# Linear attention and a gated FFN on one core: the next pair's k tiles join the projection burst, PSUM banks in shared pairs, and all transposes at the visit's end

## The chip, the cores and the metric

The kernel runs on one core of one Trainium2 chip. The metric is device time in microseconds for one execution, and the figure shown is the median of three. TensorE, VectorE, ScalarE, GpSimd and SyncE (which issues the DMAs here) each work through a list of instructions in order and wait for each other by semaphores. The profile calls them PE, DVE, ACT, POOL and SP; PEld is TensorE's weight load.

## What is computed

```python
def phi(x):
    proj = np.einsum('bhsd,df->bhsf', x, w_phi)
    proj = proj - np.max(np.abs(proj), axis=-1, keepdims=True)
    return np.concatenate([np.exp(proj), np.exp(-proj)], axis=-1)
q_p, k_p = (phi(q), phi(k))
kv = np.einsum('bhsf,bhsd->bhfd', k_p, v)
z = np.sum(k_p, axis=2)
num = np.einsum('bhsf,bhfd->bhsd', q_p, kv)
den = np.einsum('bhsf,bhf->bhs', q_p, z)[..., None] + 1e-06
attn = num / den                       # 8 batches, 8 heads, 576 tokens, 64 wide
...
h = x @ w_in                           # x: 4608 x 512, w_in: 512 x 2048
g = np.maximum(h, 0.0) + alpha * np.minimum(h, 0.0)
out = g @ w_out                        # 2048 x 512
```

There are 128 features, 256 with both signs. Everything is float32. The FFN's weights are float64, stored as pairs of words that the kernel decodes itself.

## The kernel before

**Pairs and visits.** Two heads of a batch form a pair, so there are 32 pairs. The work of a pair is cut into some 25 units (a projection, an exponential, a DMA), and a table, `places(i)`, gives each unit a number. Pair i's number plus i is the unit's place; all units of all pairs, of the FFN and of the weight decoding are sorted by place and issued in that order, which then stands on TensorE, SyncE, VectorE and ScalarE. GpSimd's order is free. The stretch between place i and i + 1 is called visit i here. The table's numbers are no times: what is fixed is the order alone.

**What TensorE does in a visit.** Of pair i: the projection of five tiles of tokens with q in them, for two heads (`project(1)`; the first of the five holds the last 64 rows of k and of q). Of pair i - 1: k_z (the sum z, by a product with ones), k_acc (kv, k features against v), the transposes of kv (`kv_turn`) and of the projected q (`q_turn`, three groups). Of pair i - 2: d (the denominator) and n (the numerator). Of pair i + 1: the projection of four k tiles (`project(0)`), behind n. From visit 9 on gemm steps of the FFN stand in between, each three matmuls (high by high, low by high, high by low, on tiles split into a rounded high part and a rest: L503 to L505 up, L509 to L511 down), and the four groups of transposes stand among those steps.

**The other engines.** VectorE takes the maximum of each projected tile over its features and subtracts it (L311, L312); this frees the PSUM bank. The part that is projected first (`pl`, two tiles 128 wide) is done ahead of the 1024-wide rest (`pj`). ScalarE takes exponentials (k: L320 and L325, q: L402 and L404), copies kv (ks), the turned kv (sf), d and n (s) out of PSUM, and does the activation of the FFN (r and g from h) and the rounding to a high part (gh); VectorE joins r and g (L240) and forms the low part (gl). VectorE inverts d; the reciprocals go to DRAM (`rec_out`), come back spread over partitions (`spread`), GpSimd multiplies (`finish`), and the result goes to x_d, from which the FFN fetches xr.

**The weights.** In the early visits one or two blocks of a weight are decoded per visit: fetched by SyncE (raww), scaled on ScalarE (L173), split on VectorE (L181 to L184), added on GpSimd, rounded and stored. `WA` holds the places of the two blocks within a visit.

**PSUM.** Eight banks while attention runs: `psf` two (h and o of the FFN; in the early visits, where there is no FFN, half of the turned q, and the k projection of pairs 0 and 1), `ps_pj` one tile of two banks (every other projection), `ps_kv` one (kv and z), `ps_m` three single banks, taken in turn by the two small projections, d, the two halves of n, the turned kv and turned q. A tile is given the next bank of its pool and waits until the bank's former tile has been read.

**After attention** a second pass over the tokens does the FFN's other 11 blocks of 128 features.

Of the kernel before, what the change touches and what calls it, by code (L numbers as in the profile page):

```python
# [36 lines left out]
W_BUFS = 2  # L37
RW_BUFS = 4
WN = 256
WA = (0.0040, 0.50)  # L40
W2A = 12.5
W2D = 0.70
G2_BUFS = 3
# [65 lines left out]
def fused_kernel(ctx: ExitStack, tc: tile.TileContext, kq, v, w_phi, w_in, w_out, alpha, out):  # L109
    nc = tc.nc  # L110
    act, dve, pool, pe = nc.scalar, nc.vector, nc.gpsimd, nc.tensor
# [94 lines left out]
    def decode_store(ff, z, o, n):  # L206
# [6 lines left out]
        scale=decode_scale,  # L213
# [50 lines left out]
    ones = cat.tile([P, 32], F32, name="ones")  # L264
    pool.memset(ones, 1.0)
    k4buf = []
    for n in range(2):
        k4 = cat.tile([P, 2, 2, FD], F32, name=f"k4_{n}")
# [3 lines left out]
    def attention_units(i):  # L272
        b, hp = divmod(i, NP)
        c = {}
# [9 lines left out]

        def project(ch):
            t = c["t", ch] = wk.tile([P, 2, 4 + ch, FD], F32, tag=f"t{ch}", name=f"t{i}_{ch}", bufs=1 + ch)
            dst, out, js = {}, [], [0, 1, 2, 3]
            if ch:
                js = [4] + js
                for h in range(2):  # L290
                    p1 = ps_m.tile([P, 1, 1, FD], F32, tag="m", name=f"pl{i}_{h}")
                    dst[h, 4] = p1[:, 0, 0]
                    out.append((slice(h, h + 1), slice(4, 5), p1))
            if ch == 0 and i < 2:
                for h in range(2):
                    p1 = psf.tile([P, 1, 4, FD], F32, tag="f", name=f"pj{i}_{ch}_{h}")
                    dst.update({(h, j): p1[:, 0, j] for j in range(4)})
                    out.append((slice(h, h + 1), slice(0, 4), p1))
            else:
                p2 = ps_pj.tile([P, 2, 4, FD], F32, tag="pj", name=f"pj{i}_{ch}")  # L300
                dst.update({(h, j): p2[:, h, j] for h in range(2) for j in range(4)})
                out.append((slice(0, 2), slice(0, 4), p2))
            for j in js:
                for h in range(2):
                    hs = slice(h * D, (h + 1) * D)
                    ts = slice((4 * ch + j) * P, (4 * ch + j + 1) * P)
                    pe.matmul(dst[h, j], lhsT=c["raw"][hs, ts], rhs=w_sb[hs], start=True, stop=True)  # L307
            for n, (hs, js, src) in enumerate(out):
                nh, nj = hs.stop - hs.start, js.stop - js.start
                m = wk.tile([P, nh, nj], F32, tag="m", name=f"m{i}_{ch}_{n}", bufs=4)  # L310
                dve.tensor_reduce(m, src, axis=AX.X, op=ALU.max, apply_absolute_value=True)  # L311
                dve.tensor_tensor(  # L312
                    t[:, hs, js], src, m.unsqueeze(3).broadcast_to([P, nh, nj, FD]), op=ALU.subtract
                )
# [39 lines left out]
                    )  # L354

        def k_z():
            c["kv"] = ps_kv.tile([P, 3, FD], F32, tag="kv", name=f"kv{i}")
            if i < ZP:
                zs = [c["x", 0][:, :, :, j, :] for j in range(4)] + [c["x", 1][:, :, :, 0, :]]
            else:  # L360
                zs = [c["z"]]
            for j, z in enumerate(zs):
                for g in range(4):
                    h, a = divmod(g, 2)
                    pe.matmul(  # L365
                        c["kv"][32 * g : 32 * g + 32, 2],
                        lhsT=ones,
                        rhs=z[:, a, h, :],
                        start=j == 0,
                        stop=j == len(zs) - 1,  # L370
                    )

        def kv_out():
            c["ks"] = st.tile([P, 3, FD], F32, tag="ks", name=f"ks{i}", bufs=1)
            act.copy(c["ks"], c["kv"])

        def kv_turn():
            ps = c["kt"] = ps_m.tile([P, 3, P], F32, tag="m", name=f"kt{i}")
            for j in range(3):
                pe.transpose(ps[:, j, :], c["ks"][:, j, :], ident)  # L380
# [5 lines left out]
        def q_turn(h):  # L386
            pp, tag = (psf, "f") if i < ZP - 1 and h < 2 else (ps_m, "m")
            ps = c["qt", h] = pp.tile([P, 2 if h == 2 else 4, P], F32, tag=tag, name=f"qt{i}_{h}")
            if h == 2:
                for g in range(2):  # L390
                    pe.transpose(ps[:, g, :], c["t", 1][:, g, 0, :], ident)
            else:
                for j in range(4):
                    pe.transpose(ps[:, j, :], c["t", 1][:, h, 1 + j, :], ident)  # L394

        def q_exp(h):
            ps = c["qt", h]
            if h == 2:
                c["qf"] = qp.tile([P, 2, 2, S], F32, tag="qf", name=f"qf{i}", bufs=QH_BUFS)
            for a, sg in enumerate((1.0, -1.0)):  # L400
                if h == 2:
                    act.activation(c["qf"][:, :, a, 4 * P :], ps[:, :, 64:], AF.Exp, scale=sg)  # L402
                else:
                    act.activation(  # L404
                        c["qf"][:, h, a, : 4 * P], ps.rearrange("p j f -> p (j f)"), AF.Exp, scale=sg
                    )

        def num():
            for u in range(2):
                ps = c["n", u] = ps_m.tile([P, HS], F32, tag="m", name=f"n{i}_{u}")  # L410
                for a in range(2):
                    for h in range(2):
                        pe.matmul(  # L413
                            ps[h * D : (h + 1) * D, :],
                            lhsT=c["st"][:, a, h * D : (h + 1) * D],
                            rhs=c["qf"][:, h, a, u * HS : (u + 1) * HS],
                            start=a == 0,
                            stop=a == 1,
                        )
# [49 lines left out]
        us = [  # L469
            (at["ld"], load),  # L470
            (at["lv"], load_v),
            (at["ka"], k_acc),
            (at["kz"], k_z),
            (at["ko"], kv_out),
            (at["kr"], kv_turn),
            (at["kc"], kv_copy),
            (at["n"], num),
            (at["d"], den),
# [9 lines left out]
        for n in range(2):  # L488
            us.append((at["p"][n], lambda n=n: project(n)))
        for n in range(3):  # L490
            us.append((at["ks"][n], lambda n=n: k_sum(n)))
            us.append((at["q"][n], lambda n=n: q_turn(n)))
# [231 lines left out]
    for ff in range(NB):  # L724
        t = T2 + ff * U2
# [75 lines left out]
```

## Time and profile before

| | us |
|---|---|
| median of three runs | 1140.24 |
| lowest, highest | 1139.62, 1142.58 |
| the profiled execution, its time | 1140.04 |
| its span | 1138.2 |
| TensorE busy | 1114.4 |
| VectorE busy | 634.0 |
| ScalarE busy | 561.1 |
| GpSimd busy | 213.9 |

The span is the time from the first to the last recorded instruction. An instruction's row gives its start, its duration, engine, line and operation, the tile written and those read, and how many like it were run together; in brackets stands the idle time before it and what ended that. TensorE's matmuls overlap, so the step from one start to the next is what one costs there. Early visits last about 10.6 us, late ones 16.5 us, of which the gemm steps are the larger half.

### The profile page before, as it was taken

To read this page: it belongs to the slowest core of one execution; us is meant where nothing else is said; L and a number is where in the kernel's file an instruction comes from. 1 tells how busy PE (TensorE), PEld (TensorE's weight loads), DVE (VectorE), ACT (ScalarE), POOL (GpSimd) and SP (SyncE) were. 2 spreads that over 40 slices of the span, in tenths; PEclk is the share of its full clock that TensorE was granted. 3 is DMA by queue.
4 is the path that set the end of the run, shared out by engine and by line. 5 is a ranking of instruction groups with operands and counts; after the bars stand their busy time and mean duration, and the time that the engine had idled before them with its cause. 6 is when DMAs were issued, how large, how long until landed. Compare 5 with 4: busy or idle time off the path is not lost.

```text
span 1138.2 us, 18351 instructions
## 1 busy us (share of the span) xinstructions
PE 1114.4 (98%) x7232; PEld 865.2 (76%) x7232; DVE 634.0 (56%) x978; ACT 561.1 (49%) x1149; POOL 213.9 (19%) x219
## 2 busy tenths in 40 slices
PE   6999999999999999999999999999999999999998
PEld 5766767777777777677778788888888888888886
DVE  7888957798687777836861342424242333333322
ACT  4777656666666765664543333333333333433332
POOL 1345332322424142243542000000000000000000
PEclk9999999999999999999999999999999999999999
DMA  5467264555556365466627030303030302112021
GB/s 190 147 186 219 68 194 143 172 164 183 162 167 195 99 211 167 146 202 219 227 65 246 32 111 1 111 1 111 1 111 1 111 1 75 37 33 79 1 74 37
DMA packets 74101, 133.68 MB, mean 117 GB/s; under 512 B 14624, under 2 KB 24480, under 8 KB 73376
## 3 DMA queue, kind: packets, MB, share of 16 engines
q1 hardware_dynamic: 71712, 122.48, 33.7%
q0 software_dynamic: 2016, 9.96, 2.5%
q8 instruction: 57, 0.93, 0.3%
q14 instruction: 28, 0.23, 0.1%
q10 hardware_dynamic: 288, 0.07, 0.0%
HBM read 93.92 MB, written 38.42 MB: 116 GB/s over the span
## 4 chain that ended last, share of the span: by engine, by line
PE 88%; DVE 6%; DMA 4%; ACT 2%; issue 1%; SPq 0%; DVEq 0%; ACTq 0%
PE h L503 11%; PE h L505 11%; PE h L504 11%; PE po L511 8%; PE po L509 8%; PE po L510 8%; PE kv L348 6%; PE n L413 5%; PE pj L307 5%; PE o L511 3%; PE o L509 3%; PE o L510 3%; PE d L431 2%; PE qt L394 2%; DMA xr<-x_d 2%; PE kv L365 1%
## 5 line engine op out<-in xcount | busy, mean ns | idle before, releaser
L240 DVE SCALAR_TENSOR_TENSOR g<-r,aln,g 128x512 f32<-128x512 f32 x144 | 111.7, 775 | 307.1 <-ACT g L236 306.9
L235 ACT ACTIVATE r<-h 128x512 f32<-128x512 f32 x144 | 86.5, 601 | 293.3 <-PE h L505 293.2
L127 DVE TENSOR_TENSOR gl<-g,gh 128x512 fp32r<-128x512 f32 x144 | 104.7, 727 | 67.6 <-ACT gh L123 67.1
L123 ACT CAST gh<-g 128x512 fp32r<-128x512 f32 x144 | 90.0, 625 | 85.6 <-DVE g L240 85.6
L236 ACT ACTIVATE g<-h 128x512 f32<-128x512 f32 x144 | 86.0, 598 | 1.0 <-DMA part_d<-os 1.0
L509 PE MATMUL po<-gh,wd 128*128 128x512 f32 x216 | 84.6, 392 | 0.7 <-ACT gh L123 0.7
L510 PE MATMUL po<-gh,wd 128*128 128x512 f32 x216 | 84.7, 392 | 0.0
L511 PE MATMUL po<-gl,wd 128*128 128x512 f32 x216 | 84.5, 391 | 0.0
L311 DVE TENSOR_REDUCE m<-pj 128x8 f32<-128x1024 f32 (+1 forms) x66 | 78.2, 1185 | 10.4 <-PE pj L307 10.3
L307 PE MATMUL pj<-w_sb,raw 64*128 64x128 f32 x1024 | 73.2, 283 | 9.8 <-DMA w_sb<-w_phi_dram 4.6
L307 PEld LDWEIGHTS pj<-w_sb,raw 64*128 64x128 f32 x1024 | 64.1, 192 | 23.3 <-issue 15.6
L189 POOL TENSOR_TENSOR aw<-ew,aw 128x256 f32<-128x256 f32 x64 | 56.6, 885 | 128.6 <-DVE ew L184 128.6
L312 DVE TENSOR_TENSOR t<-pj,m 128x1024 f32<-128x1024 f32 (+1 forms) x66 | 78.7, 1192 | 2.3
L509 PE MATMUL o<-gh,w 128*128 128x512 f32 x180 | 76.0, 422 | 2.6 <-ACT os L554 2.4
L463 POOL TENSOR_TENSOR s<-s,rr 128x576 f32<-128x576 f32 x32 | 48.5, 1517 | 145.3 <-DMA rr<-rec_d 127.7
L503 PE MATMUL h<-xh,w 128*128 128x512 f32 x180 | 75.8, 421 | 0.0
L511 PE MATMUL o<-gl,w 128*128 128x512 f32 x180 | 71.7, 399 | 3.6 <-DVE gl L127 3.4
L404 ACT ACTIVATE qf<-qt 128x512 f32<-128x512 f32 x128 | 68.4, 615 | 6.3 <-PE qt L394 6.3
L511 PE MATMUL po<-gl,w 128*128 128x512 f32 x180 | 69.7, 390 | 1.4 <-DVE gl L127 1.4
L505 PE MATMUL h<-xl,w 128*128 128x512 f32 x180 | 70.7, 393 | 0.0
L510 PE MATMUL o<-gh,w 128*128 128x512 f32 x180 | 70.6, 392 | 0.0
L504 PE MATMUL h<-xh,w 128*128 128x512 f32 x180 | 70.5, 392 | 0.0
(105 smaller groups left out, 2402.6 us busy)
## 6 DMA issues: line engine op xcount, KB each, us to landing
xr<-x_d SPq DMA_DIRECT2D x18, 1024.0 KB
raw<-kq_dram SPq DMA_DIRECT2D x31, 576.0 KB
v<-v_dram SPq DMA_DIRECT2D x32, 320.0 KB
w_d<-raww SPq DMA_DIRECT2D x38, 256.0 KB
rr<-rec_d SPq DMA_DIRECT2D x64, 144.0 KB
x_d<-s SPq DMA_DIRECT2D x32, 288.0 KB
part_d<-os SPq DMA_DIRECT2D x36, 256.0 KB
pt<-part_d SPq DMA_DIRECT2D x9, 1024.0 KB
```

What stands on the lines that cost most here:

```text
L123: return act.copy(dst, src)
L127: return eng.tensor_tensor(dst, src, f(hi), op=ALU.subtract)
L235: act.activation(st["r"], ps, AF.Relu, scale=-1.0)
L236: act.activation(st["g"], ps, AF.Relu)
L240: dve.scalar_tensor_tensor(g, st["r"], aln[:, ff : ff + 1], g, op0=ALU.mult, op1=ALU.add)
L307: pe.matmul(dst[h, j], lhsT=c["raw"][hs, ts], rhs=w_sb[hs], start=True, stop=True)
L503: pe.matmul(ps, lhsT=wt[0][:, ws], rhs=xh, start=n == 0, stop=False)
L504: pe.matmul(ps, lhsT=wt[1][:, ws], rhs=xh, start=False, stop=False)
L505: pe.matmul(ps, lhsT=wt[0][:, ws], rhs=xl, start=False, stop=n == NK - 1)
L509: pe.matmul(ps, lhsT=wt[2][:, ws], rhs=gh, start=first, stop=False)
L510: pe.matmul(ps, lhsT=wt[3][:, ws], rhs=gh, start=False, stop=False)
L511: pe.matmul(ps, lhsT=wt[2][:, ws], rhs=gl, start=False, stop=last)
```

## The change

Five things are changed; what is computed stays.

- `p`: the k projection of the next pair moves from behind n to right behind the q projection of this pair.
- PSUM: `ps_pj` gets two tiles of two banks, `ps_m` keeps one bank. The two tiles are taken in turn by the q projection, the next pair's k projection, n (both halves in one tile, so that one copy takes it out) and the turned q (or, in the early visits, the turned kv). Of the two small projections one goes to a fourth column of the kv bank, one to the bank of `ps_m`, which then also holds d and, in the late visits, the turned kv with the small part of the turned q (`kq`). The turned z goes to the fourth column of the kv bank.
- The transposes of kv and q (13) stand together behind n, in front of the visit's gemm steps.
- The q exponentials go by sign rather than by head, and earlier in the visit; VectorE's three sums of k features (`ks`) come behind both projections.
- `WA`: the second decode block of a visit moves from 0.50 to 0.0046, beside the first.

```diff
-WA = (0.0040, 0.50)
+WA = (0.0040, 0.0046)
...
-        p=(-0.9955 if early else -0.993, 0.0),
-        ke=(-0.26, 0.0011),
-        ks=(0.0015, 0.0022, 0.0026),
-        kz=1.0002,
-        ka=1.0012,
-        ko=1.0025,
-        kr=1.10,
-        kc=1.16,
-        q=(1.34, 1.50, 1.20),
-        qe=(1.46, 1.62, 1.28),
-        d=2.0004,
-        ds=2.0008,
-        n=2.005,
-        s=2.0055,
+        p=(-0.9998, 0.0),
+        kz=1.0004,
+        d=2.0006,
+        ka=1.0010,
+        n=2.0020,
+        kr=1.0030,
+        q=1.0034,
+        ds=2.0012,
+        ke=(-0.26, 0.0014),
+        ko=1.0022,
+        s=2.0028,
+        kc=1.0036,
+        qe=(1.0040, 1.0044, 1.0048) if early else (1.04, 1.30, 1.42),
+        ks=(0.02, 0.05, 0.08),
...
-    ps_m = ps_m_.enter_context(tc.tile_pool(name="ps_m", bufs=3, space=PSUM))
+    ps_m = ps_m_.enter_context(tc.tile_pool(name="ps_m", bufs=1, space=PSUM))
...
-    ps_pj = att.enter_context(tc.tile_pool(name="ps_pj", bufs=1, space=PSUM))
+    ps_pj = att.enter_context(tc.tile_pool(name="ps_pj", bufs=2, space=PSUM))
...
-                js = [4] + js
-                for h in range(2):
-                    p1 = ps_m.tile([P, 1, 1, FD], F32, tag="m", name=f"pl{i}_{h}")
...
+                kvb[i] = ps_kv.tile([P, 4, FD], F32, tag="kv", name=f"kv{i}")
+                p1 = ps_m.tile([P, 4, FD], F32, tag="m", name=f"pl{i}")
+                for h, t1 in enumerate((kvb[i][:, 3:4], p1[:, 0:1])):
+                    dst[h, 0] = t1[:, 0]
+                    out.append((slice(h, h + 1), slice(0, 1), t1.unsqueeze(1)))
+            p2 = ps_pj.tile([P, 2, 4, FD], F32, tag="pj", name=f"pj{i}_{ch}")
...
+            if i < ZP - 1:
+                c["kq"] = ps_pj.tile([P, 2, 4, FD], F32, tag="pj", name=f"kq{i}")[:, 0]
+            else:
+                c["kq"] = ps_m.tile([P, 4, FD], F32, tag="m", name=f"kq{i}")
             for j in range(3):
-                pe.transpose(ps[:, j, :], c["ks"][:, j, :], ident)
+                pe.transpose(c["kq"][:, j] if j < 2 else c["kv"][:, 3], c["ks"][:, j, :], ident)
...
-            act.copy(c["st"], c["kt"])
+            act.copy(c["st"][:, 0:2], c["kq"][:, 0:2])
+            act.copy(c["st"][:, 2], c["kv"][:, 3])
...
+            c["n"] = ps_pj.tile([P, 2, 512], F32, tag="pj", name=f"n{i}")
...
-            for u in range(2):
-                act.copy(c["s"][:, u * HS : (u + 1) * HS], c["n", u])
+            act.copy(c["s"].rearrange("p (u n) -> p u n", u=2), c["n"][:, :, :HS])
```

What the table of numbers makes of the order shows in two places. The first is TensorE at the start of visit 14; the number in a name is the pair, and h1_1_4 is a tile of the FFN. Before:

```order
L505 MATMUL h1_1_4_2486<-xl1_1_2050,w4_94 128x512
L307 MATMUL pl14_0_2492<-w_sb_73,raw14_2186 128x128
L307 MATMUL pl14_1_2493<-w_sb_73,raw14_2186 128x128
L307 MATMUL pj14_1_2494<-w_sb_73,raw14_2186 128x128 x8
L365 MATMUL kv13_2514<-z13_2338,ones_119 32x128 x4
L431 MATMUL d12_2519<-qf12_2409,sf12_2388 32x288 x8
L348 MATMUL kv13_2514<-xk13_2258,v13_2199 64x256 x8
L348 MATMUL kv13_2514<-k4_1_123,v13_2199 64x256 x2
L413 MATMUL n12_0_2552<-qf12_2409,sf12_2388 64x288 x4
L413 MATMUL n12_1_2557<-qf12_2409,sf12_2388 64x288 x4
L307 MATMUL pj15_0_2566<-w_sb_73,raw15_2377 128x128 x8
L503 MATMUL h1_1_4_2486<-xh1_1_2049,w4_94 128x512
```

And now:

```order
L302 MATMUL kv14_2432<-w_sb_73,raw14_2152 128x128
L302 MATMUL pl14_2433<-w_sb_73,raw14_2152 128x128
L302 MATMUL pj14_1_2434<-w_sb_73,raw14_2152 128x128 x8
L302 MATMUL pj15_0_2455<-w_sb_73,raw15_2337 128x128 x8
L362 MATMUL kv14_2432<-z13_2330,ones_119 32x128 x4
L436 MATMUL d12_2471<-qf12_2327,sf12_2322 32x288 x8
L343 MATMUL kv14_2432<-xk13_2204,v13_2160 64x256 x8
L343 MATMUL kv14_2432<-k4_1_123,v13_2160 64x256 x2
L419 MATMUL n12_2497<-qf12_2327,sf12_2322 64x288 x8
L380 MATMUL kq13_2510<-ident_67,ks13_2506 128x128 x2
L380 MATMUL kv14_2432<-ident_67,ks13_2506 128x128
L389 MATMUL kq13_2510<-ident_67,t13_1_2228 128x128 x2
```

The projection of pair 15's k tiles went from behind n to behind pair 14's projection, the transposes of pair 13 follow n at once, and pl14 and d12 are now tiles of one bank, as kv14 holds a small projection and then z13.

The second place is VectorE in visit 5, an early one: m is a maximum, t the subtracted projection, r9 the reciprocal of d, aw a weight block being split. Before:

```order
L311 TENSOR_REDUCE m5_1_1_831<-pl5_1_816 128x1
L312 TENSOR_TENSOR t5_1_814<-pl5_1_816,m5_1_1_831 128x128
L311 TENSOR_REDUCE m5_1_2_834<-pj5_1_817 128x8
L312 TENSOR_TENSOR t5_1_814<-pj5_1_817,m5_1_2_834 128x2x512
L450 RECIPROCAL r9_2_881<-d9_2_773 128x9
L181 TENSOR_SCALAR aw4_0_0_808<-aw4_0_0_808 128x256
```

And now:

```order
L307 TENSOR_TENSOR t5_1_799<-pl5_801,m5_1_1_816 128x128
L306 TENSOR_REDUCE m5_1_2_819<-pj5_1_802 128x8
L307 TENSOR_TENSOR t5_1_799<-pj5_1_802,m5_1_2_819 128x2x512
L306 TENSOR_REDUCE m6_0_0_832<-pj6_0_823 128x8
L307 TENSOR_TENSOR t6_0_822<-pj6_0_823,m6_0_0_832 128x1024
L455 RECIPROCAL r9_2_878<-d9_2_780 128x9
L181 TENSOR_SCALAR aw4_0_0_794<-aw4_0_0_794 128x256
```

The next pair's maximum and subtraction (m6_0, t6_0) now stand ahead of the reciprocal r9_2; before they stood behind it and behind the split of the weight block.

More of the change, by code (lines that the diff above doesn't have):

```diff
@@ L265, in fused_kernel @@
     pool.memset(ones, 1.0)
+    kvb = {}
     k4buf = []
@@ L286, in project @@
             t = c["t", ch] = wk.tile([P, 2, 4 + ch, FD], F32, tag=f"t{ch}", name=f"t{i}_{ch}", bufs=1 + ch)
-            dst, out, js = {}, [], [0, 1, 2, 3]
+            dst, out = {}, []
             if ch:
-                js = [4] + js
-                for h in range(2):
-                    p1 = ps_m.tile([P, 1, 1, FD], F32, tag="m", name=f"pl{i}_{h}")
[L292 to L303, printed above, removed]
+                kvb[i] = ps_kv.tile([P, 4, FD], F32, tag="kv", name=f"kv{i}")
[4 more added lines that the diff above has]
+            p2 = ps_pj.tile([P, 2, 4, FD], F32, tag="pj", name=f"pj{i}_{ch}")
+            dst.update({(h, ch + j): p2[:, h, j] for h in range(2) for j in range(4)})
+            out.append((slice(0, 2), slice(ch, ch + 4), p2))
+            for j in range(4 + ch):
                 for h in range(2):
@@ L356, in k_z @@
         def k_z():
-            c["kv"] = ps_kv.tile([P, 3, FD], F32, tag="kv", name=f"kv{i}")
+            if i + 1 not in kvb:
+                kvb[i + 1] = ps_kv.tile([P, 4, FD], F32, tag="kv", name=f"kv{i + 1}")
+            c["kv"] = kvb[i + 1]
             if i < ZP:
@@ L374, in kv_out @@
             c["ks"] = st.tile([P, 3, FD], F32, tag="ks", name=f"ks{i}", bufs=1)
-            act.copy(c["ks"], c["kv"])
+            act.copy(c["ks"], c["kv"][:, 0:3])
         def kv_turn():
-            ps = c["kt"] = ps_m.tile([P, 3, P], F32, tag="m", name=f"kt{i}")
+            if i < ZP - 1:
+                c["kq"] = ps_pj.tile([P, 2, 4, FD], F32, tag="pj", name=f"kq{i}")[:, 0]
+            else:
+                c["kq"] = ps_m.tile([P, 4, FD], F32, tag="m", name=f"kq{i}")
             for j in range(3):
-                pe.transpose(ps[:, j, :], c["ks"][:, j, :], ident)
+                pe.transpose(c["kq"][:, j] if j < 2 else c["kv"][:, 3], c["ks"][:, j, :], ident)
@@ L382, in kv_copy @@
         def kv_copy():
             c["st"] = st.tile([P, 3, P], F32, tag="sf", name=f"sf{i}")
-            act.copy(c["st"], c["kt"])
[L386 to L391, printed above, removed]
-            else:
+            act.copy(c["st"][:, 0:2], c["kq"][:, 0:2])
@@ new lines, in kv_copy, with q_turn @@
+            act.copy(c["st"][:, 2], c["kv"][:, 3])
+        def q_turn():
+            for g in range(2):
+                pe.transpose(c["kq"][:, 2 + g], c["t", 1][:, g, 0, :], ident)
+            if i < ZP - 1:
+                ps = [psf.tile([P, 1, 4, P], F32, tag="f", name=f"qt{i}_{h}") for h in range(2)]
+                c["qt"] = [(slice(h, h + 1), ps[h]) for h in range(2)]
+                qt = [p1[:, 0] for p1 in ps]
+            else:
+                p2 = ps_pj.tile([P, 2, 4, P], F32, tag="pj", name=f"qt{i}")
+                c["qt"] = [(slice(0, 2), p2)]
+                qt = [p2[:, h] for h in range(2)]
+            for h in range(2):
@@ L393, in q_turn, with q_exp @@
                 for j in range(4):
[L394 to L398, printed above, removed]
+                    pe.transpose(qt[h][:, j], c["t", 1][:, h, 1 + j, :], ident)
+        def q_exp(n):
+            if n == 0:
                 c["qf"] = qp.tile([P, 2, 2, S], F32, tag="qf", name=f"qf{i}", bufs=QH_BUFS)
[L400 to L406, printed above, removed]
+                for a, sg in enumerate((1.0, -1.0)):
+                    act.activation(c["qf"][:, :, a, 4 * P :], c["kq"][:, 2:4, 64:], AF.Exp, scale=sg)
+                return
+            a, sg = ((0, 1.0), (1, -1.0))[n - 1]
+            for hs, ps in c["qt"]:
+                act.activation(
+                    c["qf"][:, hs, a, : 4 * P], ps.rearrange("p h j f -> p h (j f)"), AF.Exp, scale=sg
+                )
@@ L408, in num @@
         def num():
+            c["n"] = ps_pj.tile([P, 2, 512], F32, tag="pj", name=f"n{i}")
             for u in range(2):
-                ps = c["n", u] = ps_m.tile([P, HS], F32, tag="m", name=f"n{i}_{u}")
                 for a in range(2):
```

4 lines of the change are left out of this document (2 added, 2 removed).

## The prediction

> **What bounds the kernel now.** I read the page first, then TensorE's own list of waits, then one late visit instruction by instruction.
>
> ```profile
> span 1138.2 us, 18351 instructions
> PE 1114.4 (98%) x7232; PEld 865.2 (76%) x7232; DVE 634.0 (56%) x978; ACT 561.1 (49%) x1149; POOL 213.9 (19%) x219
> L311 DVE TENSOR_REDUCE m<-pj 128x8 f32<-128x1024 f32 (+1 forms) x66 | 78.2, 1185 | 10.4 <-PE pj L307 10.3
> L312 DVE TENSOR_TENSOR t<-pj,m 128x1024 f32<-128x1024 f32 (+1 forms) x66 | 78.7, 1192 | 2.3
> ...
> PE o L511 <- DVE gl L127: 3.4, 5, 1.6
> PE d L431 <- ACT qf L404: 1.0, 2, 0.7
> ```
>
> TensorE is busy for 98% of the span, and its waits (total, times, longest) are small: 3.4 us on low halves, 1.0 us on d. VectorE's maximum and subtraction of a 1024-wide projection cost 1.2 us each, which is used below. Since TensorE sets the time, any new wait of it is paid in full, and only what shortens its own list of work is a gain. Here is visit 19 on TensorE:
>
> ```profile
> 276.27 0.49 PE L307 MATMUL pl<-w_sb,raw 64*128 64x128 f32 x4
> 276.59 1.06 PE L307 MATMUL pj<-w_sb,raw 64*128 64x128 f32 x16
> 277.58 0.43 PE L365 MATMUL kv<-z,ones 128*32 128x128 f32 x8
> 277.82 1.15 PE L431 MATMUL d<-qf,sf 128*32 128x288 f32 x16
> 278.91 1.95 PE L348 MATMUL kv<-xk,v 128*64 128x256 f32 x16
> ...
> 281.12 2.11 PE L413 MATMUL n<-qf,sf 128*64 128x288 f32 x16
> 283.16 1.16 PE L307 MATMUL pj<-w_sb,raw 64*128 64x128 f32 x16
> 284.25 0.50 PE L509 MATMUL o<-gh,w 128*128 128x512 f32 x1
> 284.58 0.39 PE L510 MATMUL o<-gh,w 128*128 128x512 f32 x1
> 284.81 0.39 PE L511 MATMUL o<-gl,w 128*128 128x512 f32 x1
> 285.05 0.49 PE L380 MATMUL kt<-ident,ks 128*128 128x128 f32 x3
> 285.29 0.48 PE L509 MATMUL o<-gh,w 128*128 128x512 f32 x1
> ...
> 287.68 0.60 PE L394 MATMUL qt<-ident,t 128*128 128x128 f32 x4
> 288.04 0.48 PE L509 MATMUL o<-gh,w 128*128 128x512 f32 x1
> ```
>
> The step from one start to the next is the price of a row, since the matmuls overlap.
>
> **The late visits' packing (visits 10 to 30, 21 of them).** By these starts the first projection burst costs 0.32 + 0.99 = 1.31 us, z 0.24, d 1.09, k_acc 2.21 (278.91 to 281.12), n 2.04, the next pair's projection 1.09. Put behind the first burst, the second projection costs 0.99 as its equal there does, 0.10 less than alone; n then goes straight into the transposes. The four groups of transposes are one of three (0.24, 285.05 to 285.29), two of four (0.36 each, 287.68 to 288.04) and one of two, which at the same 0.08 apiece makes 0.16: 1.12 us. Each also makes the next L509 step longer: after other work it is 0.33 (284.25 to 284.58), where a gemm step among its like takes 0.23 (284.58 to 284.81). Four such restarts are 0.40, 1.52 together. In the early visits, where 13 already stand in a row, they take 1.57 us (52.85 to 54.42, below), no less than the 1.52 here. What is saved is the 0.10 at the second projection and the restart of 0.10 behind it (284.25 to 284.58): before 1.09 + 0.10 + 1.52 = 2.71, after 0.99 + 1.57 + 0 to 0.10 for the one restart, 2.56 to 2.66. Were a transpose 0.09 in the row, as in the group of four, it would be 2.26. I take a saving near the first, 0.13 a visit: 21 x 0.13 = **-2.8 us** (ends 0.06 and 0.21 a visit, -1.3 and -4.4). The low-half waits of 3.4 us come about when a short run of gemm steps stands between transposes; longer runs give VectorE more time in some of them: **-1.0** (0 to -2).
>
> **The new wait.** The trace of before has no such wait. The pool of single banks ps_m goes from three banks to one. Before, a visit's two small projections (pl) and d took three banks, and the first to need an old one was n, 3.3 us later (277.82 to 281.12). Now pl and d lie in the same bank, and the other small tile lies in the kv bank, whose z columns TensorE writes next. So d cannot start until VectorE has taken the maximum of the second small tile and subtracted it. TensorE reaches z at burst start + 1.31 + 0.99 = 2.30 and d at 2.30 + 0.24 = 2.54. VectorE's end in before, with the burst's start on TensorE in the row ahead:
>
> ```profile
> 117.03 0.49 PE L307 MATMUL pl<-w_sb,raw 64*128 64x128 f32 x4
> 120.24 0.29 DVE L312 TENSOR_TENSOR t<-pl,m 128x128 f32<-128x128 f32 x1
> 134.93 0.49 PE L307 MATMUL pl<-w_sb,raw 64*128 64x128 f32 x4
> 138.51 0.29 DVE L312 TENSOR_TENSOR t<-pl,m 128x128 f32<-128x128 f32 x1
> 190.67 0.49 PE L307 MATMUL pl<-w_sb,raw 64*128 64x128 f32 x4
> 194.61 0.29 DVE L312 TENSOR_TENSOR t<-pl,m 128x128 f32<-128x128 f32 x1
> 309.31 0.49 PE L307 MATMUL pl<-w_sb,raw 64*128 64x128 f32 x4
> 312.62 0.29 DVE L312 TENSOR_TENSOR t<-pl,m 128x128 f32<-128x128 f32 x1
> 425.56 0.49 PE L307 MATMUL pl<-w_sb,raw 64*128 64x128 f32 x4
> 428.55 0.29 DVE L312 TENSOR_TENSOR t<-pl,m 128x128 f32<-128x128 f32 x1
> 442.08 0.49 PE L307 MATMUL pl<-w_sb,raw 64*128 64x128 f32 x4
> 446.45 0.29 DVE L312 TENSOR_TENSOR t<-pl,m 128x128 f32<-128x128 f32 x1
> ```
>
> End minus burst start: 3.50, 3.87, 4.23, 3.60, 3.28 and 4.66 us in visits 10, 11, 14, 21, 28 and 29. Less 2.54 these are waits of 0.96, 1.33, 1.69, 1.06, 0.74 and 2.12, together 7.9; with 0.05 each for the signal **+8.2 us**. The other visits end early enough or miss by 0.3 at most. Queued behind d on TensorE stand k_acc, n, the transposes and all gemm steps of the visit, so nothing fills the gap. What makes VectorE late is seen in visit 14:
>
> ```profile
> 189.53 2.04 ACT L325 ACTIVATE xk<-t 128x1024 f32<-128x1024 f32 x2
> 192.42 0.64 ACT L236 ACTIVATE g<-h 128x512 f32<-128x512 f32 x1
> 193.10 0.75 DVE L240 SCALAR_TENSOR_TENSOR g<-r,aln,g 128x512 f32<-128x512 f32 x1 [1.49 <-ACT g L236]
> ```
>
> VectorE stands 1.49 us for ScalarE's g, which is queued behind the k exponentials of 2.04 us; the small maxima stand behind that g in VectorE's order. After the change the same g stands ahead of the same small maxima, and the k exponentials at the same place ahead of it. The q exponentials move up, but their transposes now stand in front of all gemm steps, so the h tile that ScalarE works on comes up to 1.4 us later: the two cancel, and I keep the lateness. Ends: +4 (half of it goes) and +14 (0.3 more in each of the 21 visits).
>
> The Trainium skill ("Perfetto Trace Analysis", section Optimizing Tensor Performance, Matmuls) asks that independent matmul groups rotate through different PSUM banks, so that the evacuation of one overlaps the matmuls of the next. It speaks against going from three banks to one; read strictly it would charge every visit. By the rows only the late ones pay.
>
> **The early visits (0 to 8) and the start.** No gemm covers anything there, so the order on the other queues matters too.
>
> ```profile
> 43.84 0.49 PE L307 MATMUL pl<-w_sb,raw 64*128 64x128 f32 x4
> 48.98 0.32 SPq L453 DMA_DIRECT2D rec_d<-r  x1
> 52.85 0.55 PE L380 MATMUL kt<-ident,ks 128*128 128x128 f32 x3
> 54.42 0.49 PE L307 MATMUL pl<-w_sb,raw 64*128 64x128 f32 x4
> 58.95 0.44 ACT L173 ACTIVATE aw<-raww 128x256 f32<-128x256 f32 x1 [0.23 <-DMA raww<-w_in_dram]
> ```
>
> A visit takes 10.58 us (43.84 to 54.42). TensorE's part shrinks by 0.10 at the merged burst and 0.10 where k_acc runs into n: 6 x 0.2 = -1.2 for visits 3 to 8, and at the start, where the first pairs' banks are shared otherwise, about -0.4. Against it: the k projection's maximum and subtraction move ahead of the reciprocal on VectorE, so rec_d, issued at visit start + 5.14 (48.98), goes out after the small tiles (1.7 us) and twice 2.4 us (the two page rows), with the reciprocal at about + 6.75, 1.6 us later. SP's queue is in order: the fetch of raw behind rec_d, the spread and the weight fetch all shift by as much. The first weight tile lands 9.97 after rec_d (48.98 to 58.95), now at the next visit's start + 6.1 to 6.3 (6.75 + 9.97 less 10.4 to 10.6). ScalarE's scaling of both weight tiles (0.44 for the first) stands ahead of the d copy, the k exponentials and the kv copy, on which the transposes wait; these start at + 9.0 before (43.84 to 52.85) and at about + 8.8 now. That the two decode blocks of a visit now follow each other takes ScalarE and VectorE work out of the visit's middle and costs TensorE nothing while the first arrives in time. The sum of gain and delay could be -2.5 (the gain and half as much again) or +5 (0.8 in each of six visits); I take **0**, since the some 2.6 us left to ScalarE there are about what its pieces need (two scalings 0.4 each, an exponential pair and two copies).
>
> The second pass (after 35.4 on the table) has the same order on each engine and costs nothing new. The one n copy in place of two, and two copies of the turned kv in place of one, are off TensorE's path: they need to end before the q burst of the next visit, and until then TensorE has the gemm steps (284.25 onward) to do.
>
> **Sum:** -2.8 - 1.0 + 8.2 + 0 = +4.4 us on the profiled 1140.04. That execution is 0.2 under the median of the runs, 1140.24, so the forecast is **1144.6 us**.
>
> **The rivals.**
> A, the forecast: d waits for VectorE in the late visits. 1144.6, with 1142 to 1150 as its own range. Chance 0.45.
> B, VectorE is on time: the q exponentials, earlier by up to 0.2 of a visit, empty ScalarE's queue ahead of the k exponentials, and the small maxima start within 1.26 us of the burst (2.54 less the 1.13 that four pieces of 0.28 to 0.29 take, and 0.15 for the signals). For it: in visits not listed they do that already. Against it: in visit 14 ScalarE's queue is full from the h tiles, which come later now. Then -2.8 - 1.0 and the early -1.6: 1140.2 - 5.4 = 1134.8. It decides from half of the listed visits being on time onward. Chance 0.18; faster.
> C, half of the waits stay, 4.1 us, and the early visits gain half, 0.8: 1140.2 - 3.8 - 0.8 + 4.1 = 1139.7; with no gain there 1140.5. No change. Chance 0.27.
> D, the early visits are paced by SP's chain: rec_d 1.6 later delays weights or raw beyond the slack, about 0.8 a visit for six visits and about 1.6 in visit 8, together 6.4 us on top of half to all of A: 1146.9 to 1151, say 1150. For it: ScalarE already waits for raww at 58.95. Chance 0.10; slower.
>
> A measurement of this kernel can tell 0.3%, 3.4 us, from no change. Faster takes B, 0.18; same takes C, 0.27; slower takes A and D, 0.55. The range reaches from B's edge to D's middle: 1135.5 to 1151.5.
>
> **What would show it.** In TensorE's list of waits after the change: d waiting for t (VectorE) some 6 to 9 times, 8 us in total, longest near visit 29. The burst of projections 2.30 us long in a late visit; transposes in one row of 1.2 to 1.6 us; late visits without a d wait some 0.13 us shorter. rec_d at visit start + 6.75 and early visits of 10.4 to 10.6. Wrong would be: no d waits over 0.3 us (B), or early visits over 11 us or visit 8 over 15 us (D), or a loss at a transposed tile that waits for its copy, which I priced at nothing.

## The result, and the profile after

The changed kernel takes 1146.46 us (median of 20 executions, 1142.92 to 1154.52), the kernel before 1140.28 (20 executions, 1138.04 to 1144.16): a ratio of 1.0054, with a 95% interval of 1.004 to 1.0069. The forecast was 1144.6 us and slower; the range held the time. The profiled execution took 1143.3 us, 3.3 more than the one of before, at a span of 1141.5.

The page of the changed kernel and TensorE's list of its waits (total, times, longest):

```profile
span 1141.5 us, 18286 instructions
PE 1110.7 (97%) x7232; PEld 870.2 (76%) x7232; DVE 630.7 (55%) x974; ACT 555.0 (49%) x1101; POOL 209.8 (18%) x219
```

```profile
PE kv L362 <- DVE t L307: 6.9, 7, 1.9
PE pj L302 <- DMA w_sb<-w_phi_dram: 4.1, 1, 4.1
PE pj L302 <- DMA raw<-kq_dram: 2.8, 1, 2.8
PE o L514 <- ACT os L559: 2.3, 3, 1.7
PE pj L302 <- DVE t L307: 1.9, 1, 1.9
PE d L436 <- DVE t L307: 1.5, 8, 0.2
...
PE o L516 <- DVE gl L127: 0.8, 2, 0.5
```

The first row is z waiting for VectorE to read the small projection in its bank, the sixth d waiting for the other one: 6.9 + 1.5 = 8.4 us that the kernel before did not have. Its waits on low halves went from 3.4 to 0.8. New is also a stand (idle time of TensorE) of 2.8 us for raw.

Visit 19, the one shown of before, without its gemm rows, on TensorE of the changed kernel:

```profile
278.63 0.37 PE L302 MATMUL pl<-w_sb,raw 64*128 64x128 f32 x1
...
278.95 1.95 PE L302 MATMUL pj<-w_sb,raw 64*128 64x128 f32 x32
280.83 0.43 PE L362 MATMUL kv<-z,ones 128*32 128x128 f32 x8
281.08 1.15 PE L436 MATMUL d<-qf,sf 128*32 128x288 f32 x16
...
284.37 2.11 PE L419 MATMUL n<-qf,sf 128*64 128x288 f32 x16
286.41 0.44 PE L380 MATMUL kq<-ident,ks 128*128 128x128 f32 x2
...
287.01 1.04 PE L400 MATMUL qt<-ident,t 128*128 128x128 f32 x8
287.81 0.48 PE L514 MATMUL o<-gh,w 128*128 128x512 f32 x1
...
294.82 0.37 PE L302 MATMUL pl<-w_sb,raw 64*128 64x128 f32 x1
```

The burst takes 2.20 us (278.63 to 280.83), the 13 transposes 1.40 (286.41 to 287.81), the visit 16.19; before it took 16.52.

The stretches of the span around two of the stands show what was not in the forecast at all. Each row has the busy times of TensorE, its weight loads, VectorE, ScalarE and GpSimd, then the granted clock, the share of the DMA engines and GB/s:

```profile
86.00:88.00 2.00, 0.72 (x14) 0.53 (x10) 1.93 (x5) 2.00 (x6) 0.00 (x0) 1.00 1.06 422
88.00:90.00 2.00, 0.48 (x4) 0.51 (x6) 1.35 (x2) 2.00 (x4) 0.00 (x0) 0.88 1.04 298
90.00:92.00 2.00, 2.00 (x28) 1.74 (x29) 0.37 (x1) 0.42 (x1) 1.32 (x1) 0.50 0.97 324
92.00:94.00 2.00, 2.00 (x48) 1.61 (x44) 1.90 (x2) 1.40 (x3) 2.00 (x4) 0.76 0.44 163
446.00:448.00 2.00, 0.59 (x12) 0.35 (x16) 1.93 (x6) 0.00 (x0) 0.00 (x0) 0.98 0.89 146
448.00:450.00 2.00, 2.00 (x18) 0.67 (x14) 1.97 (x3) 0.00 (x0) 1.21 (x1) 0.50 0.93 369
450.00:452.00 2.00, 2.00 (x14) 1.20 (x16) 1.97 (x3) 1.02 (x3) 0.19 (x1) 0.66 0.16 53
```

After the stand for raw in visit 8 and the one of 1.92 us at z in visit 29 TensorE works at half clock for 3.41 us. Weighted by the rows, each stretch is worth 1.7 us of full-clock time (2.00 x 0.12 + 2.00 x 0.50 + 2.00 x 0.24 for the first). There is a third at 14 to 18 us. The profiled execution of before has none: its granted clock is 1.00 throughout. Over all 20 executions of the changed kernel the mean clock is 0.9946; over the 23 of the kernel before that were run beside the first experiments, 0.9985.

### The profile page after: what moved, and what is told of

Its sections match the earlier page's. It is cut to its first block, busy times and chain, and to the rows that moved or that the text cites. A ratio compares the mean times of both kernels' runs of the same rounds, so it can differ in the third digit from the quotient of the medians.

```text
span 1141.5 us, 18286 instructions
## 1 busy us (share of the span) xinstructions
PE 1110.7 (97%) x7232; PEld 870.2 (76%) x7232; DVE 630.7 (55%) x974; ACT 555.0 (49%) x1101; POOL 209.8 (18%) x219
## 4 chain that ended last, share of the span: by engine, by line
PE 53%; DMA 4%; DVE 2%; ACT 1%; issue 1%; POOL 0%; SPq 0%; ACTq 0%; POOLq 0%; DVEq 0%
PE h L510 8%; PE h L508 8%; PE h L509 8%; PE po L516 8%; PE po L514 8%; PE po L515 8%; DMA part_d<-os 1%; PE o L516 1%; DMA xr<-x_d 1%; PE o L514 1%; PE o L515 1%; PE kv L343 1%; PE n L419 1%; DMA rec_d<-r 1%; DMA rr<-rec_d 1%
## 5 line engine op out<-in xcount | busy, mean ns | idle before, releaser
L307 DVE TENSOR_TENSOR t<-pj,m 128x1024 f32<-128x1024 f32 x64 | 78.4, 1225 | 3.8
L306 DVE TENSOR_REDUCE m<-pj 128x8 f32<-128x1024 f32 x64 | 77.8, 1215 | 3.3 <-PE pj L302 3.3
L302 PE MATMUL pj<-w_sb,raw 64*128 64x128 f32 x1024 | 67.6, 282 | 11.2 <-DMA w_sb<-w_phi_dram 4.1
L514 PE MATMUL o<-gh,w 128*128 128x512 f32 x180 | 71.9, 399 | 2.4 <-ACT os L559 2.3
L508 PE MATMUL h<-xh,w 128*128 128x512 f32 x180 | 71.3, 396 | 0.0
L515 PE MATMUL o<-gh,w 128*128 128x512 f32 x180 | 70.3, 391 | 0.0
L509 PE MATMUL h<-xh,w 128*128 128x512 f32 x180 | 70.2, 390 | 0.0
L515 PE MATMUL po<-gh,w 128*128 128x512 f32 x180 | 70.0, 389 | 0.0
```

The lines of the kernel that those rows point to most:

```text
L508: pe.matmul(ps, lhsT=wt[0][:, ws], rhs=xh, start=n == 0, stop=False)
L509: pe.matmul(ps, lhsT=wt[1][:, ws], rhs=xh, start=False, stop=False)
L514: pe.matmul(ps, lhsT=wt[2][:, ws], rhs=gh, start=first, stop=False)
L515: pe.matmul(ps, lhsT=wt[3][:, ws], rhs=gh, start=False, stop=False)
```

## The experiments

The ratios below are to the kernel before, run on the same chip beside each group. The changed kernel itself stands at 1.0054.

**Small pieces first.** VectorE's order alone: a join or a low half in the last 0.15 of a visit goes behind the small pieces (the last line below takes the 1024-wide ones after them).

```diff
+                    if behind and t % 1 > 0.85 and t < NPAIR - 2:
+                        t = t // 1 + 1 + 0.00003 + 0.00001 * (t % 1)
...
+                us.append((at["p"][n] + 0.00006, lambda: reduce_out(3)))
```

> Changed kernel, with one edit on VectorE alone: where a join (g) or a low half (gl) of the FFN stands in the last 0.15 of a visit, it is moved behind the two small maxima and subtractions of the next visit, but stays ahead of the 1024-wide ones. TensorE's order is the same. Theory (z and d wait for the small pieces, which wait in VectorE's order for ScalarE's g): TensorE's waits of z and d on t, 8.4 us in the changed kernel's profile (6.9 + 1.5), fall to under 2 us, the half-clock stretch of visit 29 goes with its pause, and the time falls by 6 to 10 us to about 1138. Rival (the small pieces are late for another reason, the projection itself or the bank): the waits stay at 7 to 8 us and the time stays within 2 us of 1146.

Measured: 0.9986 (0.9972 to 1.0001), 0.7% or 7.8 us under the changed kernel. TensorE's waits, where the edit left them:

```profile
PE pj L302 <- DMA raw<-kq_dram: 3.5, 1, 3.5
...
PE kv L372 <- DVE t L317: 1.4, 3, 1.0
...
PE d L446 <- DVE t L317: 0.6, 3, 0.2
```

The 8.4 us are 2.0, and the half-clock stretch of visit 29 is gone. So the loss at z and d comes from the order on VectorE, where the small pieces stood behind a g that waits for ScalarE. It is not the bank itself: TensorE's order and the banks are the same in this run.

**xr behind raw.** `FL0` from 2.20 to 2.11, which puts the fetch of pair 9's raw ahead of the 1 MB of xr.

> Changed kernel, with the first fetch of xr (1 MB) issued behind the fetch of raw for pair 9 instead of ahead of it; nothing else. Theory (in visit 8 TensorE stands 2.80 us for raw, then works at half clock for about 4 us, which costs another 2): the wait of pj on raw is gone, the clock around 88 to 94 us stays 1.00, visit 8 lasts about 10.5 instead of 14.9, and of these 4 us some 0 to 1.5 come back as ScalarE's wait for xr at the cast; time 2.5 to 4.5 us lower, 1142 to 1144. Rival (the weights or d9 limit visit 8 in any case): less than 1 us lower.

Measured: 1.0041 (1.0026 to 1.0057), about 0.13% under the changed kernel by the two ratios, whose intervals overlap. The stand for raw in visit 8 fell from 2.80 to 0.50 us and its half-clock stretch went, as the theory has it. But the visit only went from 14.87 to 14.20, since ScalarE now stood for xr in front of the kv copy, and TensorE behind it:

```profile
PE kq L380 <- ACT ks L372: 3.1, 1, 3.1
```

The expectation for visit 8 (10.5 us) was wrong: the stand moved by one transfer.

**Reciprocal first.** `dv` and `rd` of the early visits from 3.0016 and 3.0017 to 3.0001 and 3.00015, between the two projections' work.

> Changed kernel, with the reciprocal and rec_out of the early visits placed between the two projections' work on VectorE, so that rec_d, raw and the weight fetch behind it on SyncE's queue go out some 2.4 us earlier. Theory: the stand for raw in visit 8 shrinks from 2.80 to about 0.4 and its half-clock stretch goes; the other early visits stay at 10.2 to 10.8, since they had slack; time 3 to 4 us lower, 1142 to 1143.5. Rival (VectorE has no room there, the k projection comes late instead): visits 2 to 7 grow by 0.2 or more each, and the time is the same or higher.

Measured: 1.0018 (1.0007 to 1.003). In visit 7 the reciprocals' DMA went out 4.2 us after the visit's start instead of 6.7, but raw, behind it in the queue, went out only 0.6 us earlier than in the changed kernel (82.52 for 83.14). SyncE's queue in that run, and what xr waited for:

```profile
78.45 0.33 SPq L471 DMA_DIRECT2D x_d<-s  x1
78.89 0.37 SPq L458 DMA_DIRECT2D rec_d<-r  x1
82.03 0.38 SPq L524 DMA_DIRECT2D xr<-x_d  x1
82.52 0.43 SPq L280 DMA_DIRECT2D raw<-kq_dram  x1
```

```profile
SPq L524 <- DMA x_d<-s: 2.7, 1, 2.7
```

xr is issued 3.1 us behind rec_d, though it is next in the queue, since it waits until the write of x_d, issued at 78.45, has landed; raw stands behind xr. xr went out at 82.03 here, 3.6 us after that write, and at 82.65 in the changed kernel, 3.5 us after it. The stand for raw fell only to 2.30 us. So it is the write of x_d that makes raw late there, not the late reciprocal. The time did fall, by 0.36%, to where the theory had it, but not by the theory's path. The mean clock was 0.9962 for 0.9946; which of its parts made the gain was not settled.

**Decode block back.** `WA` back to (0.0040, 0.50).

> Changed kernel, with the second decode block of a visit back at its old place in the middle of the visit (0.50). Theory (priced at nothing): within 1 us of the changed kernel. Rival (the two blocks together delay ScalarE or VectorE in visits 4 and 7, which last 10.64 and 10.77 instead of 10.23): 0.5 to 1 us lower and those two visits at 10.2 to 10.3. Other rival (the second block in the middle delays the exponentials in front of the transposes, now that all transposes come at once): early visits longer by 0.3 each, 2 us higher.

Measured: 1.0389 (1.0366 to 1.0413), 38 us slower than the changed kernel, which neither the theory nor its two rivals came near. In each of visits 2 to 9 TensorE stands 2.6 to 4.5 us at z. VectorE at the start of visit 6 of that run, whose burst began at 85.40:

```profile
87.89 0.29 DVE L181 TENSOR_SCALAR aw<-aw 128x256 uint32<-128x256 uint32 x1 [6.26 <-ACT aw L173]
88.22 1.56 DVE L182 SCALAR_TENSOR_TENSOR aw<-raww,aw 128x256 uint32<-128x256 uint32 x1
89.88 0.63 DVE L183 TENSOR_SCALAR ew<-aw 128x256 uint32<-128x256 uint32 x1
90.55 0.43 DVE L184 SCALAR_TENSOR_TENSOR ew<-raww,ew 128x256 f32<-128x256 uint32 x1
90.89 0.28 DVE L306 TENSOR_REDUCE m<-kv 128x1 f32<-128x128 f32 x1
```

The second block's split stands ahead of the small maxima and waits 6.26 us for ScalarE's scaling; z waits for all of it. Moving the decode is what keeps the new dependence cheap in the early visits.

**Decode block moved alone**, in the kernel before: `WA` = (0.0040, 0.0046) and nothing else.

> The kernel before, with one part of the change alone: the second decode block of a visit beside the first (0.0046). Theory (its place matters only where z and d wait for the small pieces; in the kernel before they do not): within 2 us of the kernel before. Rival (the decode in the middle of the visit cost the kernel before something too): 2 to 6 us faster. Third: the two blocks in a row hold up ScalarE in front of the transposes, 1 to 5 us slower.

Measured: 1.0222 (1.0209 to 1.0236), 26 us slower, where the worst expected was 5. The parts do not add up one by one: the same edit costs 26 us in the kernel before, and taking it out of the changed kernel costs 38. Without the early k projection VectorE's work on k comes late in the visit (from 57.81 us in visit 4), the second split stands behind it (from 60.21) and runs past the next burst's start (61.35), and with it come late the small pieces and ScalarE's q exponentials, which stand behind the rounding of that block. The rounding waits for GpSimd's sum, and d for the exponentials:

```profile
64.08 0.40 ACT L123 CAST w<-aw 128x256 fp32r<-128x256 f32 x1 [2.60 <-POOL aw L189]
```

```profile
PE d L431 <- ACT qf L404: 11.3, 12, 4.4
```

Visits 3 to 7 take 11.9 to 13.2 us there for 10.6. Where the rest of the 26 us goes stays open.

**k projection back behind n**, with small pieces first: `p` = (-0.9975, 0.0).

> The changed kernel with small pieces first, and the next pair's k projection back behind n (in front of the transposes). Theory: the burst is 1.31 us instead of 2.30, so z and d are reached 0.99 earlier and wait in nearly every visit, d until about 1.7 us after the burst's start (0.1 to 0.2 of wait in each of 21 late visits, more in the visits that were late), and the second projection costs 0.10 to 0.20 more alone; late visits 16.4 to 16.55, time 4 to 9 us above small pieces first alone. Rival (the place of the k projection does not matter, only the banks and the transposes do): within 1.5 us of it.

Measured: 1.0829 (1.0814 to 1.0844), 96 us over small pieces first alone, where 4 to 9 were expected. The wait at z is 4.2 us in most early visits and up to 4.9 in late ones, and the mean clock is 0.9676. The list of waits, and VectorE in visit 4, whose burst began at 56.87:

```profile
PE kv L372 <- DVE t L317: 56.5, 19, 4.9
```

```profile
57.89 0.28 DVE L181 TENSOR_SCALAR aw<-aw 128x256 uint32<-128x256 uint32 x1
...
61.01 0.83 DVE L184 SCALAR_TENSOR_TENSOR ew<-raww,ew 128x256 f32<-128x256 uint32 x1
61.76 0.28 DVE L316 TENSOR_REDUCE m<-kv 128x1 f32<-128x128 f32 x1
...
72.51 1.22 DVE L316 TENSOR_REDUCE m<-pj 128x8 f32<-128x1024 f32 x1 [7.11 <-PE pj L302]
```

VectorE stands 7.11 us in the middle of the visit for the k projection, and the two splits behind it push the small maxima of the next visit to 61.76, 4.9 us after the burst's start. The early place of the k projection is worth far more on VectorE than the 0.1 to 0.2 us on TensorE by which it was priced.

**Transposes in two groups among the gemm steps**, with small pieces first (late visits: `kr` 1.10, `q` 1.20, `kc` 1.16, `qe` from 1.28).

> The changed kernel with small pieces first, and in the late visits the transposes in two groups among the gemm steps (one of 3, one of 10) instead of in one row behind n. Theory (a row of its own saves restarts): one more restart, so a late visit without a wait takes 16.29 instead of 16.19; about 2 us more than small pieces first alone. Rival (the row saves nothing, the 0.33 us come from the projection burst): 16.19 within 0.03, same time.

Measured: 1.0102 (1.0085 to 1.0119), 13 us over small pieces first alone. Several late visits without a wait take 16.29 us, 0.10 more, as the theory has it for one restart. The other 11 us were not foreseen:

```profile
PE kq L399 <- ACT sf L394: 10.8, 7, 2.0
```

The second group writes the bank that ScalarE's copy of the turned kv still reads. In one row the transposes are all done before that copy begins. What is saved by the row is thus also a wait on the shared bank.

**Pauses on purpose.** With small pieces first, in visits 18 to 25 VectorE takes the 1024-wide maximum and subtraction, or the maximum alone, ahead of the small pieces.

> The changed kernel with small pieces first, but in the eight visits 18 to 25 VectorE takes the 1024-wide maximum and subtraction ahead of the small ones, so that z and d find the small pieces late on purpose: a stand of about 2.0 us plus 0.3 at d in each. Theory A (a stand of 2 us between a projection burst and z also lowers the granted clock behind it): half-clock stretches of 3 to 5 us in most of these eight visits, each visit 4 to 4.5 us longer than 16.19, the time 30 to 36 us above small pieces first alone. Theory B (the stands alone cost; the half-clock stretches come from something else): clock 1.00 there, visits at 18.3 to 18.6, 17 to 19 us above.

> As the run with pauses of two, but in visits 18 to 25 only the 1024-wide maximum (1.2 us) stands ahead of the small pieces: a stand of about 0.95 us plus 0.3 at d. Theory A (the clock falls only where the stand is long enough; 0.72 to 1.41 us did not do it in the profiles so far): clock 1.00 in these visits, each 1.0 to 1.3 us longer than 16.19, 8 to 10 us above small pieces first alone. Rival (any stand at this place can do it): half-clock stretches in some of them, 14 us or more above.

Measured: 1.0295 (1.0273 to 1.0317) and 1.0094 (1.0076 to 1.0112), that is 35 us and 12 us above small pieces first alone. In each of the eight visits the stand at z was 2.21 to 2.23 us in the one and 0.96 to 0.97 in the other. The windows around visit 18, first with the long pause, then with the short one:

```profile
264.00:266.00 2.00, 0.20 (x8) 0.16 (x8) 1.93 (x5) 0.73 (x2) 0.00 (x0) 1.00 0.00 0
266.00:268.00 2.00, 1.81 (x26) 0.62 (x20) 1.90 (x3) 0.01 (x1) 0.00 (x0) 0.77 0.64 175
268.00:270.00 2.00, 2.00 (x10) 1.11 (x12) 1.90 (x3) 1.01 (x3) 1.22 (x1) 0.50 0.90 325
270.00:272.00 2.00, 2.00 (x18) 1.22 (x16) 2.00 (x2) 0.42 (x1) 1.12 (x1) 0.87 0.99 347
```

```profile
264.00:266.00 2.00, 0.94 (x17) 0.53 (x21) 1.93 (x6) 1.05 (x3) 0.03 (x1) 1.00 0.01 0
266.00:268.00 2.00, 2.00 (x26) 1.10 (x20) 1.90 (x3) 1.02 (x3) 0.00 (x0) 1.00 0.51 124
268.00:270.00 2.00, 2.00 (x20) 1.24 (x18) 2.00 (x2) 0.48 (x1) 0.05 (x1) 1.00 0.85 224
```

With the long pause the clock fell in eight visits of eight, with the short one in none. (The eight are not independent; see the last section.) A visit with the long pause takes 20.51 us, 4.32 more than 16.19: 2.2 at z, some 0.2 at d, and 1.9 by the clock. So here a stand of about 2 us cost nearly twice its length. The short one costs 1.4 us a visit, somewhat more than expected, at full clock.

**Small pieces first and xr, with later casts.** `FL0` 2.11 and the four casts of the first xr at 0.95 to 0.35 ahead of the gemm.

> The changed kernel with VectorE's small pieces first (as in the run before), the first fetch of xr behind raw, and now also ScalarE's four casts of that xr later (their places 0.35 to 0.95 of a visit ahead of the first gemm instead of 0.45 to 1.80). Theory (visit 8 is long because ScalarE and TensorE stand for a DMA, raw or xr, and the fall of the clock behind that stand costs as much again): visit 8 comes down from 16.9 to 10.3 to 11.5 us, without a half-clock stretch around 90 us, and the time is 4 to 7 us under that of small pieces first alone (0.9986 of the kernel before), near 0.994. Rival (the lost time moves on to visit 9, where the casts now press): visit 9 grows by 3 or more, and the gain is under 2 us.

Measured: 0.9977 (0.9967 to 0.9987). Visit 8 came down from 16.92 to 12.48 us at full clock, less far than expected. But visit 9 took 1.5 more and visit 11 2.7 more: in visit 11 TensorE stands for os, because ScalarE stands 5.5 us for the second xr.

```profile
PE o L526 <- ACT os L571: 4.6, 3, 3.6
```

This time the 3.6 us at that place were followed by a half-clock stretch (155.4 to 158.8), worth 1.7 of the 2.7 us.

**The later casts for every xr** (`FX` = (0.70, 0.58, 0.46, 0.35)), added to the last.

> Small pieces first, xr behind raw with later casts (as before), and now the four casts of every later xr at places 0.70 to 0.35 of a visit ahead of the first gemm instead of 0.95 to 0.35. Theory (in visit 11 TensorE stands 3.6 us for os, because ScalarE stands 5.5 us for the second xr in front of it): that stand goes or falls under 1 us, with its half-clock stretch; time 3 to 6 us under the run with small pieces and xr (0.9977), near 0.994. Rival (xr lands too late for the gemm itself): the stand moves to the first up step of the next chunk, and the time is the same.

Measured: 0.9937 (0.9922 to 0.9952), a median of 1133.64 us against 1140.87 before. The list of waits has for os only

```profile
PE o L526 <- ACT os L571: 0.8, 2, 0.7
```

and the mean clock of its executions is 0.998. This version beats both kernels.

**The start back in the FFN's two banks**, added to that: the k projections of pairs 0 and 1 as in the kernel before.

> As the run with all casts later, and the k projections of pairs 0 and 1 back in the FFN's two banks as in the kernel before (one bank for each head), so that the start does not share the two tiles. Theory (the start lost 1.2 to 1.9 us up to the first full visit, 23.0 to 23.7 against 21.8, through a stand of 1.9 for the shared tile and the half clock behind it): visit 2 begins at 21.8 to 22.2, 1 to 2 us faster. Rival (the stand of about 2 us stays, since before also stood 2.1 us there, and only the chance of the clock differs between executions): within 0.7 us.

Measured: 0.9931 (0.9918 to 0.9944), no difference from the last that these intervals tell. The stand moved from the shared tile (1.9 us) to z (2.13 us at 14.04), and the half clock came there. The rival was right.

## Why the prediction was right, and where it was not

The side was right, and the forecast 1.9 us off, but not every term was the size it was given.

- **The wait at z and d: +8.2, measured 8.4.** It fell in visits 10, 11, 14, 21, 28 and 29, all of those named, and also in 17 (0.9 us) and 26 (0.3); the longest is in 29. The size is right partly by luck: visits 10 and 28 waited about half of what was worked out, and 17 and 26 made up for it. Most of it also falls one step earlier than forecast, at z (6.9) and not at d (1.5), since z waits for the other small tile. That VectorE's lateness would stay as the trace of before shows it was right, and small pieces first shows the cause by moving that order alone.
- **Packing: -0.13 a late visit, measured -0.33** (16.52 to 16.19): the term was mis-sized. The 13 transposes in a row take 1.40 us here, not the 1.57 read from an early visit, and the burst 2.20, not 2.30. Over 21 visits that would be -6.9 in place of -2.8. The prediction had a saving of 0.45 worked out for a cheaper transpose (2.26 for 2.71), and left it outside its ends. The two-group run gives 0.10 for one restart, as worked out.
- **Low halves: -1.0, measured -2.6** (3.4 to 0.8), a little over the end of the range given.
- **The early visits and the start: 0.** Six visits (2 to 7) together take 62.3 us for 64.3 (-2.0; the gain was put at -1.2, for visits 3 to 8), visit 8 1.8 more, the start 1.2 more. The sum is near what was taken, but the step that feared the late reciprocal is wrong: rec_d did move to 6.66 us after a visit's start as worked out (6.75), yet the early visits got shorter, and in visit 8 it was xr ahead of raw, waiting for x_d, that held raw back, not rec_d, as reciprocal first showed.
- **That moving the decode block costs nothing** held only for the whole change. Alone it costs 26 us, left out it costs 38. The step looked at where TensorE would wait with the block moved, but not at what VectorE's order would be without it.
- **The clock: not in the sum at all.** This is the term that was missing. In the profiled execution three stretches are worth about 5 us. Over the executions the mean clock fell from 0.9985 to 0.9946; a line through the 20 executions of the changed kernel (time against clock) gives 0.94 us for each 0.001, so some 3.7 of the 6.2 us go with it. That is a fit to scattered points (correlation 0.80), not a measured part. The wait was priced at its length, where a stand of 2 us can cost nearly double.

Without the clock, packing and low halves (-9.5) would have paid for the wait (+8.4). That the forecast came out close is partly luck: two mistakes of opposite sign, 5.7 us too little gain and no price for the clock. Rival B (VectorE on time) was what small pieces first made: 0.9986, only 1.6 us under the kernel before, while the clock of its executions stayed low (0.9945); in its profile the half-clock stretches stand at the start and in visit 8. Rival D had a loss in visit 8 as it said, by another cause.

## What to carry to other kernels

Where a PSUM bank is handed from one use to the next within a few microseconds, its price is the order on the engine that reads it: look at what stands ahead of that read, and put it first. Price a stand of TensorE by what it does to the clock behind it as well as by its length: here stands of one length cost that length alone or 1.7 us more, by where they fell. So look at the spread of the executions and their clocks, not only at one profile. Parts of a change that share an engine's order cannot be priced one at a time: two edits here cost 26 to 96 us alone or left out, and the whole change 6.

## What was not expected of the hardware

Whether a stand halves TensorE's granted clock depends here on how it falls into fixed windows of 3.41 us, and not on its length alone. In every profile the half-clock stretches start a whole number of 3.413 us apart (in the changed kernel at 14.44, 89.53 and 447.93 us, 22 and 105 times 3.413 apart), and except at the very end each lasts 3.41 or 6.83 us. Counted in these windows over the 14 profiles, from the first record of the clock on (7 to 20 us), each of the 49 full-clock windows in which TensorE was idle for 1.92 us or more was followed by one at half clock. So were 8 of the 22 with 1.6 to 1.91 us, and none of the other 4527. Below are the two windows around the stand of 2.44 us at os in the kernel before, and then the two around the stand of 1.92 us at z in visit 29 of the changed kernel:

```profile
148.19:151.60 3.41, 1.98 (x11) 1.37 (x9) 0.00 (x0) 0.14 (x1) 0.00 (x0) 1.00 1.07 329
151.60:155.02 3.42, 2.40 (x11) 2.00 (x12) 0.22 (x1) 3.42 (x7) 2.40 (x2) 1.00 0.61 171
444.51:447.93 3.42, 1.31 (x28) 0.88 (x28) 2.57 (x7) 0.75 (x2) 0.00 (x0) 1.00 0.59 106
447.93:451.34 3.41, 3.41 (x24) 1.51 (x25) 3.34 (x4) 1.02 (x3) 1.40 (x1) 0.50 0.63 249
```

A window's edge cuts the longer stand, so that TensorE is idle for 1.43 us in one window and 1.02 in the next, and the clock stays. The shorter one lies in one window, idle for 2.11 us, and the next is at half clock. In the same way the 3.1 us behind n in the run with xr behind raw left 1.76 and 1.38 us, and the clock at 1.00. A stand of 1.92 us at z in the run with the k projection back (at 437.25 us), cut into windows idle for 0.83 and 1.28 us, left it at 1.00 as well.

So the long pause's eight of eight count as one trial: its visits of 20.51 us are 6.01 windows long, and all eight stands lie at nearly the same part of a window. What the same pause costs elsewhere in a window was not tried. What decides between 1.6 and 1.91 us stays open. The Trainium skill (TensorE: Matmul & The Clock Gate, Part 1) has the clock come down after an idle window of about 3.4 us and says that this window runs freely. The traces agree with windows of that length. That these run freely would also explain why the mean clock differs between executions of one kernel (0.989 to 1.000 for the changed one), but as one execution of each was profiled, it is not shown. The window need not be idle throughout: 1.92 of its 3.41 us were enough.
